# Linear attention with a gated feed-forward on one core: the sums of phi(k) apart from v, w1 and w2 loaded by columns, another order of steps

## The chip, the cores and the metric

The kernel runs on one core of a Trainium2 chip. The metric is the device time of one execution in microseconds (us). Differences of about 2% are what a measurement of this kernel tells from none. Five engines work side by side, each through its own queue of instructions in order: TensorE (PE) multiplies matrices and writes PSUM; VectorE (DVE) and ScalarE (ACT) compute elementwise; GpSimd (POOL) and SyncE (SP) are used here mainly to issue transfers.

## The reference

```
phi(x) = (x if x > 0 else exp(x) - 1) + 1
q_p, k_p = phi(q), phi(k)                     # (8, 8, 576, 64) each
kv  = einsum('bhsd,bhse->bhde', k_p, v)
z   = sum(k_p, axis=2)
att = einsum('bhsd,bhde->bhse', q_p, kv) / (einsum('bhsd,bhd->bhs', q_p, z) + 1e-06)
x   = att with heads joined                   # (4608, 512)
out = ((x @ w1) * (x @ w2) @ w3) @ w_out      # w1, w2: 512x1024, w3: 1024x1024, w_out: 1024x512
```

Inputs and output are float32; the kernel multiplies in bfloat16.

## The kernel before

**Work.** First w3 and w_out are multiplied into one matrix, w_f: for each of eight 128-row pieces of w3, eight transposes on PE (`wt`, L193), a copy out of PSUM (`wc`, L197), eight matmuls with w_out (`wm`, L203) and a copy to bf16 (`wd`, L207). For each batch, q, k and v are loaded in f32 into tiles `raw` of one pool with five buffers, which w3 shares. phi is an exp on ScalarE (`x`, L217), a max and add (`y`, L221) and a min (`z`, L228) on VectorE. v is cast to bf16 next to a column of ones (`vc`, L234), so that one K step (`kv_mm`, L247) gives kv and z together.

**Two ways through attention.** Batches 0 and 1 transpose q on PE (`qa`, `qb`), spread kv and z over 64 columns (`kvz_copy`, L328), multiply both with q (`e`, L339), take the reciprocal as exp(-ln) on ScalarE (`er`, L347 and L348) and multiply (`em`, L352), which leaves x transposed in `xt`. Their last 64 rows go by `rm` and `rd`. Batches 2 to 7 transpose q by DMA (`T`, L260), multiply (`A`, L272: nd), divide (`G`, L290 to L294) and transpose the result into `xt` by DMA (`D`, L306).

**Feed-forward.** The 4608 rows make nine chunks of 512. For each chunk c and each of eight feature blocks f, `g` multiplies x with w1 (a) and w2 (b), four 128-row pieces of the contraction each (L388); ScalarE copies a out of PSUM (`fc`, L399), VectorE multiplies it with b (`fm`, L406 or L408). `O` multiplies with w_f (L416), `oc` copies (L420), `S` stores (L427). The last output piece (`Q`) goes in two parts (L438, L439).

**Order.** A string of steps is written out by hand or by a planner; each step is issued as it stands, and each engine keeps that order. `g0.3.1.0` is chunk 0, block 3, w2, first half of the contraction. A plus sign takes VectorE instead of ScalarE for a copy, and POOL's queue instead of SP's for a load.

**Transfers.** POOL issues the loads that change the type, and in the first stage all of them; eight of its transfers may be in flight, the ninth waits for the first. SP issues later loads, DMA transposes and stores, also eight in flight. A load also waits until its buffer is given back.

**PSUM.** Four buffers of one bank (`mm_ps`) serve w_f, a, b and O; two of two banks (`at_ps`) serve the transposes and attention.

Of the kernel before, what the change touches and what calls it, by code (L numbers as in the profile page):

```python
# [9 lines left out]
F32 = mybir.dt.float32  # L10
# [57 lines left out]
"""


@with_exitstack
def kernel(
# [45 lines left out]
    zero = consts.tile([P, NCH], BF16)  # L118

# [10 lines left out]
    def constants(part):  # L130
        if part == 0:
            make_identity(nc, ident)
        elif part == 1:
            for t in vts:
                nc.vector.memset(t[:, :, :, :, D:D + 1], 1.0)
            nc.vector.memset(eps, 1e-6)
        elif part == 2:
# [14 lines left out]
    def load_qkv(name, src, b, part, pool):  # L152
        if (name, b) not in raw:
            raw[name, b] = ld.tile([P, 4, HW], F32, tag="ld", name=f"{name}32")
        hs = slice(2 * part, 2 * part + 2) if part < 2 else slice(0, 4)
        (nc.gpsimd if pool else nc.sync).dma_start(
            out=raw[name, b][:, hs, :],
            in_=src[b].rearrange("(hp u) (p j) d -> (u p) hp (j d)", u=2, j=NJ)[:, hs, :])
# [79 lines left out]
    def kv_mm(b, cs):  # L238
        if 0 in cs:
            kvps[b] = at_ps.tile([P, 2, NCH], F32, tag="at", name="kvp")  # L240
        kk, vt = ph["k", b], vts[b % 2]
        for c in cs:
            for j in range(NJ):
                for u in range(2):
                    rows = slice(u * R, (u + 1) * R)
                    for a in range(2):
                        nc.tensor.matmul(  # L247
                            kvps[b][a * D:(a + 1) * D, u, c * (D + 1):(c + 1) * (D + 1)],
                            kk[rows, c, j, a, :], vt[rows, c, j, a, :],
                            start=(j == 0), stop=(j == NJ - 1))  # L250
# [73 lines left out]
    def kvz_copy(b, z, alt):  # L324
        t = kvz[b, z] = att.tile([P, 2, 2, D], BF16, tag="kvz", name="kvz", bufs=2)
        src = kvps[b][:, :, 0:2 * (D + 1)].rearrange("p u (c e) -> p u c e", e=D + 1)
        src = src[:, :, :, D:D + 1].to_broadcast([P, 2, 2, D]) if z else src[:, :, :, 0:D]
        copy_of(alt)(out=t, in_=src)  # L328
# [16 lines left out]
    def first_recip(b, c, a):  # L345
        r = rcs[b, c, a] = sm.tile([P, NCH], F32, tag="a_sb", name="rc")
# [98 lines left out]
    def step(s):  # L445
# [32 lines left out]
        elif op == "K":  # L478
            kv_mm(x, (0, 1) if y == 2 else (y,))
        elif op == "kc":  # L480
# [13 lines left out]
        elif op == "kz":  # L494
            kvz_copy(x, y, alt)
# [60 lines left out]
```

## Time and profile before

| what | value |
|---|---|
| median of 3 runs | 252.36 us (252.0 to 255.04) |
| the profiled execution's own time | 252.82 us |
| its span | 251.0 us |
| PE busy | 234.2 us, 93% |
| DVE busy | 152.0 us, 61% |
| ACT busy | 119.7 us, 48% |
| POOL busy | 22.0 us, 9% |
| read from HBM, written | 38.80 MB, 9.44 MB |
| granted PE clock, mean | 0.984 |

The span runs from the first to the last recorded instruction; the time is somewhat longer than the span, since it holds what lies around it. A busy PE isn't PE at its peak, since its matmuls overlap.

### The profile page before, as it was taken

What the parts mean: (1) busy time and instruction counts of PE and PEld (TensorE: products, weight loads), DVE (VectorE), ACT (ScalarE), POOL (GpSimd) and SP (SyncE); (2) the same over time, 40 slices, a digit from 0 to 9 for tenths busy, and PEclk for the clock granted to TensorE, in tenths of its full rate; (3) what the DMA queues carried; (4) which work ended last, traced back from release to release, by engine and by line L of the source; (5) the groups of instructions that cost most, each with busy time, mean ns of one, the idle gap of its engine ahead of it and who ended that gap; (6) DMA issues with size and microseconds to landing.
All of it is one profiled execution on the core that took longest, in us unless ns stands there. A gap on an engine that the chain in (4) does not pass through costs nothing.

```text
span 251.0 us, 4536 instructions
## 1 busy us (share of the span) xinstructions
PE 234.2 (93%) x1799; PEld 112.6 (45%) x1816; DVE 152.0 (61%) x285; ACT 119.7 (48%) x171; POOL 22.0 (9%) x39
## 2 busy tenths in 40 slices
PE   6599888999888999979999999999999999999993
PEld 2255434453443445434444544454444444444442
DVE  0239676987677888686688893576136435633411
ACT  2008898689667773363568773311131233013320
POOL 8651641100000000000000000000000000000000
PEclk9589999999999999999999999999999999999999
DMA  5999999998999997996999942589601201161025
GB/s 101 195 304 386 227 329 336 369 305 160 360 396 188 365 305 154 316 220 147 375 308 343 376 108 73 62 152 138 209 24 33 93 0 55 61 201 42 3 78 131
DMA packets 47796, 50.36 MB, mean 201 GB/s; under 512 B 30496, under 2 KB 30752, under 8 KB 47776
## 3 DMA queue, kind: packets, MB, share of 16 engines
q1 hardware_dynamic: 42272, 34.12, 51.1%
q0 software_dynamic: 5360, 15.86, 22.1%
q8 instruction: 14, 0.23, 0.4%
q10 hardware_dynamic: 144, 0.10, 0.1%
q14 instruction: 6, 0.05, 0.1%
HBM read 38.80 MB, written 9.44 MB: 192 GB/s over the span
## 4 chain that ended last, share of the span: by engine, by line
PE 74%; DMA 17%; issue 2%; ACT 2%; POOL 2%; DVE 1%; SPq 0%; DVEq 0%; ACTq 0%; POOLq 0%
PE b_ps L388 22%; PE a_ps L388 21%; PE o_ps L416 21%; DMA w_sb<-in_moe_w_dram 6%; PE wf_ps L203 5%; DMA q<-in_q_dram 5%; DMA xt<-xn 3%; DMA wo<-in_moe_w_out_dram 3%; PE nd L272 3%; PE kvp L247 2%; ACT e L217 1%; DMA out_dram<-o_sb 1%; PE w3p L193 1%; DVE xt L352 1%; POOL w3b L182 0%
## 5 line engine op out<-in xcount | busy, mean ns | idle before, releaser
L388 PEld LDWEIGHTS <-w_sb 128*128 128x128 bf16 x576 | 54.4, 98 | 67.3 <-issue 4.5
L388 PE MATMUL a_ps<-xt,w_sb 128*128 128x512 bf16 x288 | 70.9, 379 | 2.7 <-DMA xt<-xn 1.4
L388 PE MATMUL b_ps<-xt,w_sb 128*128 128x512 bf16 x288 | 70.2, 379 | 1.2 <-DMA w_sb<-in_moe_w_dram 0.8
L399 ACT COPY a_sb<-a_ps 128x512 f32<-128x512 f32 x72 | 41.7, 584 | 60.1 <-PE a_ps L388 44.1
L408 DVE TENSOR_TENSOR ab<-a_sb,b_ps 128x512 bf16<-128x512 f32 x64 | 45.5, 729 | 32.0 <-ACT a_sb L399 16.9
L416 PE MATMUL o_ps<-wf_sb,ab 128*128 128x512 bf16 x267 | 63.1, 379 | 0.7
L416 PEld LDWEIGHTS <-ab 128*128 128x128 bf16 x280 | 26.8, 98 | 31.8 <-issue 0.6
L217 ACT ACTIVATE e<-k 128x1152 bf16<-128x1152 f32 x16 | 18.1, 1160 | 20.2 <-PE wf_ps L203 16.8
L420 ACT COPY o_sb<-o_ps 128x512 f32<-128x512 f32 x20 | 11.7, 584 | 32.8 <-PE o_ps L416 26.6
L420 DVE COPY o_sb<-o_ps 128x512 f32<-128x512 f32 x15 | 10.3, 690 | 16.6 <-PE o_ps L416 10.2
L217 ACT ACTIVATE e<-q 128x1152 bf16<-128x1152 f32 x16 | 18.1, 1160 | 4.8 <-DMA q<-in_q_dram 3.3
L203 PE MATMUL wf_ps<-wo,w3t 128*128 128x512 bf16 x61 | 16.0, 411 | 1.0 <-DVE w3t L197 0.5
L294 DVE TENSOR_TENSOR xn<-nd,r 128x512 bf16<-128x512 f32 x24 | 15.4, 685 | 0.0
L221 DVE TENSOR_SCALAR r<-k 128x1152 bf16<-128x1152 f32 x16 | 11.9, 751 | 4.2 <-DMA k<-in_k_dram 4.2
L234 ACT CAST vt<-v 128x1152 bf16<-128x1152 f32 x10 | 11.6, 1172 | 2.8 <-PE kvp L247 1.6
L221 DVE TENSOR_SCALAR r<-q 128x1152 bf16<-128x1152 f32 x16 | 11.9, 751 | 0.2
L228 DVE TENSOR_TENSOR k<-e,r 128x1152 bf16<-128x1152 bf16 x16 | 11.8, 748 | 0.0
L228 DVE TENSOR_TENSOR q<-e,r 128x1152 bf16<-128x1152 bf16 x16 | 11.8, 751 | 0.0
L272 PE MATMUL nd<-kvb,qt 128*128 128x130 bf16 (+1 forms) x120 | 10.6, 222 | 1.0 <-DVE xnr L294 1.0
L272 PEld LDWEIGHTS <-qt 128*128 128x128 bf16 (+1 forms) x120 | 8.3, 100 | 7.1 <-issue 2.1
L197 DVE COPY w3t<-w3p 128x1024 bf16<-128x1024 bf16 x6 | 4.0, 688 | 11.8 <-PE w3p L193 11.8
L406 DVE TENSOR_TENSOR ab<-a_sb,b_ps 128x512 bf16<-128x512 f32 x8 | 5.5, 687 | 8.3 <-PE b_ps L388 7.5
(53 smaller groups left out, 128.8 us busy)
## 6 DMA issues: line engine op xcount, KB each, us to landing
out_dram<-o_sb SPq DMA_DIRECT2D x70, 128.0 KB, 2.1
k<-in_k_dram SPq DMA_DIRECT2D x5, 1152.0 KB, 6.4
v<-in_v_dram SPq DMA_DIRECT2D x5, 1152.0 KB, 9.6
q<-in_q_dram SPq DMA_DIRECT2D x5, 1152.0 KB, 10.3
k<-in_k_dram POOLq DMA_DIRECT2D x4, 576.0 KB, 10.6
q<-in_q_dram POOLq DMA_DIRECT2D x4, 576.0 KB, 10.4
v<-in_v_dram POOLq DMA_DIRECT2D x4, 576.0 KB, 13.5
w3b<-in_moe_w_dram POOLq DMA_DIRECT2D x8, 256.0 KB, 9.0
```

The costliest lines, as they stand in the source:

```text
L203: nc.tensor.matmul(wfs[i], w3ts[i][:, kc, :], wos[0][:, kc, :], start=(kc == 0), stop=(kc == FC - 1))
L217: nc.scalar.activation(out=es[name, b, c], in_=raw[name, b][:, 2 * c:2 * c + 2, :], func=AF.Exp)
L221: nc.vector.tensor_scalar(out=rs[name, b, c], in0=raw[name, b][:, 2 * c:2 * c + 2, :], scalar1=0.0, scalar2=1.0, op0=ALU.max, op1=ALU.add)
L228: nc.vector.tensor_tensor(out=ph[name, b][:, c].rearrange("p j a d -> p a j d"), in0=es[name, b, c].rearrange("p a (j d) -> p a j d", j=NJ ...
L234: copy_of(alt)(out=vts[b % 2][:, c, :, :, 0:D].rearrange("p j a d -> p a j d"), in_=raw["v", b][:, 2 * c:2 * c + 2, :].rearrange("p a (j d ...
L272: nc.tensor.matmul(nd[0:n, u, 2 * c * (D + 1):2 * (c + 1) * (D + 1)], w, kvb[b % 2][:, u, c].rearrange("p a e -> p (a e)"), start=True, st ...
L294: nc.vector.tensor_tensor(out=dst.rearrange("p (i u) e -> p u i e", u=2), in0=v4[:, :, :, 0:D], in1=r[0:n].unsqueeze(3).to_broadcast([n, 2 ...
L388: nc.tensor.matmul(fps[c, f, w], (w1_sb, w2_sb)[w][:, kc, f * P:(f + 1) * P], xt[:, 4 * c:4 * c + 4, kc, :], start=(first and n == 0), sto ...
L399: nc.scalar.copy(out=fsb[c, f], in_=fps[c, f, 0])
L408: nc.vector.tensor_tensor(out=abs_[c][:, f].rearrange("p (m t g) -> p m g t", g=2, t=R), in0=fsb[c, f].rearrange("p (m g t) -> p m g t", g ...
L416: nc.tensor.matmul(o_pss[c, m], abs_[c][:, f, m * P:(m + 1) * P], wf_sb[:, f, :], start=(f == 0), stop=(f == FC - 1))
L420: copy_of(alt)(out=o_sbs[c, m], in_=o_pss[c, m])
```

## The change

1. For batches 0 and 1 (`SUMS_FIRST`) v is loaded as bf16 by the transfer itself, and its cast (`vc`) is gone. K uses it as it lies in the raw tile, with 64 columns instead of 65.
2. The sums z are computed by a step of their own, `Z` (36 matmuls for each half batch against a tile of ones), which needs k only. `kvz_copy` is split into halves (`kz b.z.c`), z from the new sums' PSUM tile, kv from K's.
3. The reciprocals of batches 0 and 1 lie in the tiles of `xn` instead of the small pool `a_sb`.
4. w1 and w2 are loaded in halves of columns (features 0 to 511, then 512 to 1023) instead of halves of rows.
5. The order is a new one from end to end. At its head q of batch 0 comes first, its first half on SP's queue, with 9, 11 and 1 warm-up matmuls instead of 10, 4 and 6; chunk 0 works blocks 0 to 3, then 4 to 7. Later K, A, G and D of batches 2 to 7 stand at other places, and k and v of batch 4 are loaded ahead of batch 3.

```diff
+    ones = consts.tile([P, D], BF16)
...
+            if name == "v" and b in SUMS_FIRST:
+                raw[name, b] = raw[name, b].bitcast(BF16).rearrange("p h x -> p (h x)")[:, 0:4 * HW].rearrange(
+                    "p (h x) -> p h x", h=4)
...
     def load_w12(x, y):
-        kcs = slice(2 * y, 2 * y + 2)
+        fs = slice(y * NCH, (y + 1) * NCH)
         nc.gpsimd.dma_start(
-            out=(w1_sb, w2_sb)[x][:, kcs, :],
-            in_=(moe_w1, moe_w2)[x].rearrange("(c p) n -> p c n", p=P)[:, kcs, :])
+            out=(w1_sb, w2_sb)[x][:, :, fs],
+            in_=(moe_w1, moe_w2)[x].rearrange("(c p) n -> p c n", p=P)[:, :, fs])
...
-        kk, vt = ph["k", b], vts[b % 2]
+        kk = ph["k", b]
+        if b in SUMS_FIRST:
+
+            n, vt = D, raw["v", b].rearrange("p (c a) (j d) -> p c j a d", a=2, j=NJ)
+        else:
+            n, vt = D + 1, vts[b % 2]
...
+    def z_mm(b, c):
+
+        if b not in zps:
+            zps[b] = at_ps.tile([P, 2, NCH], F32, tag="at", name="zp")
+        kk = ph["k", b]
+        for j in range(NJ):
+            for u in range(2):
+                rows = slice(u * R, (u + 1) * R)
+                for a in range(2):
+                    nc.tensor.matmul(zps[b][a * D:(a + 1) * D, u, c * D:(c + 1) * D],
+                                     kk[rows, c, j, a, :], ones[rows], start=(j == 0), stop=(j == NJ - 1))
+
+    def kvz_copy(b, z, c, alt):
+        if (b, z) not in kvz:
+            kvz[b, z] = att.tile([P, 2, 2, D], BF16, tag="kvz", name="kvz", bufs=2)
+        cs = slice(c, c + 1) if c < 2 else slice(0, 2)
+        if z and b in zps:
+            src = zps[b][:, :, 0:2 * D].rearrange("p u (c e) -> p u c e", e=D)[:, :, cs]
...
+        copy_of(alt)(out=kvz[b, z][:, :, cs], in_=src)
```

The head of the two orders (loads `l`, with `w` for w1 and w2, `e` for w3, `o` for w_out):

```
before  i2 i1 le6 lo1 H10 le0 lo0 le7 le3 lo3 i0 lo2 wt6 le5 wt0 wc6+ lk0.1+ wc0+ lq0.0+ wm6.0.4 i3 wm0.0.4 le1 ...
        ... lw0.1 ... lw0.0 ... lk1.0+ ... lq1.0+ ... lw1.0 ... lk1.1+ ... lw1.1 ...
after   i2 lq0.0 le2 i1 lo0 H9 i0 i3 lo1 le3 le6 le0 wt2 H11 lo2 wc2+ xq0.0 lo3 yq0.0 le1 zq0.0 lk0.0+ qa0.0 le5 ...
        ... lw0.0 ... lk1.1+ ... lk1.0+ ... lw1.0 ... lq1.0+ ... lw0.1 ... lq1.1+ ... lw1.1 ...
```

Places in the new order that the prediction speaks of:

```
... e1.0.0 er1.1.1 em1.1.0 O0.3 em1.0.1 xq2.1 em1.0.0 O0.0 ... zq2.0 xk2.1 S0.0 g1.1.0.1 ... fc1.1 ...
... A3.2 fm2.0 A3.3 xq4.1 O1.3 G3.1 xq4.0 O2.2 oc1.3 D2.2 yq4.0 D3.1 ... O2.3 ... g3.7.0.2 ...
... S1.2 kc4.1+ fc3.3 zq5.0 A4.1 A4.0 g3.2.1.2 G4.0 T5.0 ... D4.0 ... g4.2.0.2 ...
```

More of the change, by code (lines that the diff above doesn't have):

```diff
@@ new lines @@
+wm6.4.8 lv0.1+ wd2+ wt1 wd6+ wm0.4.8 lw0.0 wc1 yk0.0 wm3.4.8 xk0.0 wd0+ lk1.1+ wt5 wd3+ wm1.0.4 wc5 zk0.0
+lk1.0+ wm1.4.8 xk0.1 yk0.1 wm5.0.4 wd1+ wm5.4.8 zk0.1 lw1.0 xq0.1 Z0.0 wd5+ Z0.1 lq1.0+ yq0.1 kz0.1.0 wt4
+kz0.1.1 wc4+ e0.0.1 lw0.1 er0.0.1 zq0.1 wt7 wm4.0.4 wc7+ lq1.1+ er0.0.0 wm4.4.8 qa0.1 lw1.1 wd4 K0.0 qb0.1+
+wm7.0.4 kz0.0.0+ e0.1.1 e0.0.0 er0.1.0 K0.1 em0.0.0 wm7.4.8 em0.0.1 lv1.1+ kz0.0.1 er0.1.1 e0.1.0 wd7+
+g0.2.0.0 em0.1.0 g0.1.0.0 lv1.0+ g0.0.0.0 xk1.1 em0.1.1 rm0 g0.3.0.0 yk1.1 rd0 lq2.2+ g0.2.0.1 yk1.0
@@ new lines @@
+er1.1.1 em1.1.0 O0.3 em1.0.1 xq2.1 em1.0.0 O0.0 yq2.0 oc0.3 xq2.0 S0.3 yq2.1 g1.1.1.0 em1.1.1 g1.1.0.0 oc0.0
+g1.0.1.0 zq2.0 xk2.1 S0.0 g1.1.0.1 g1.7.0.0 zq2.1 g1.7.0.1 fc1.1 g1.1.1.1 yk2.1 T2.0 rm1 fc1.7 fm1.1
+g1.4.0.0 xk2.0 g1.6.1.0 zk2.1 g1.7.1.0 rd1 g1.4.0.1 T2.1 vc2.1+ g1.6.1.1 g1.0.1.1 fc1.4 yk2.0 g1.7.1.1 vc2.0
+g1.6.0.0 zk2.0 g1.6.0.1 lk4.2 fm1.7 K2.0 fc1.6 lv4.2 K2.1 fm1.6 g1.2.0.0 lk3.2 kc2.0 g1.3.0.0 kc2.1+
+g1.4.1.0 A2.0 A2.1 g1.2.0.1 G2.0 g1.4.1.1 fc1.2 g1.3.0.1 g1.2.1.0 fc1.3 g1.2.1.1 g1.3.1.0 fm1.4 A2.2 A2.3
@@ new lines @@
+zq5.0 A4.1 A4.0 g3.2.1.2 G4.0 T5.0 g3.0.0.2 g3.3.1.2 fm3.2 D4.0 K5.0 K5.1 fm3.3 fc3.0 g3.6.1.2 S1.3 kc5.0
+fm3.0 A4.2 g3.7.1.2 kc5.1+ S2.1 A4.3 fm3.7 g3.6.0.2 T5.1 G4.1 g4.2.0.2 fc3.6 g4.2.1.2 fc4.2 g4.5.0.2 lv6.2
+fm4.2 g4.3.0.2 lq6.2 fc4.5 fm3.6 g4.0.0.2 lk6.2 fc4.3 O3.1 fc4.0 A5.0 oc3.1+ O3.0 A5.1 oc3.0 g4.1.0.2 G5.0
+S3.1 g4.5.1.2 vc6.0 g4.0.1.2 D4.1 fm4.5 g4.3.1.2 fm4.0 fc4.1 g4.6.0.2 D5.0 fm4.3 xq6.1 A4.4 g4.6.1.2 G4.2
+g4.7.1.2 fc4.6 yq6.0 xq6.0 O3.3 yq6.1 lq7.2 xk6.0 fm4.6 g4.1.1.2 oc3.3+ lk7.2 xk6.1 A5.4 O3.2 fm4.1 S3.3
@@ new lines @@
+G5.2 g4.7.0.2 D4.2 oc3.2 zq6.0 g5.7.0.2 vc6.1+ fc4.7 g5.4.0.2 yk6.1 fc5.7 A5.2 fm4.7 fc5.4 g4.4.0.2 D5.2
+zq6.1 g4.4.1.2 fc4.4 zk6.1 T6.1 xq7.0 g5.3.0.2 fm4.4 g5.3.1.2 xq7.1 yq7.0 O4.2 yq7.1 T6.0 fc5.3 zq7.0 xk7.1
+O4.3 fm5.3 oc4.2 S3.2 yk7.1 xk7.0 zq7.1 g5.7.1.2 S4.2 zk7.1 oc4.3 g5.2.0.2 fm5.7 g5.2.1.2 S4.3 fc5.2 yk7.0
+g5.6.0.2 fm5.2 S3.0 g5.5.1.2 fc5.6 zk7.0 g5.4.1.2 lv7.2 yk6.0 A5.3 g5.0.0.2 fm5.4 T7.1 zk6.0 O4.1 fc5.0 G5.1
+T7.0 g5.0.1.2 g5.5.0.2 fm5.0 K6.0 fc5.5 D5.1 oc4.1+ K6.1 g5.6.1.2 fm5.5 kc6.1 S4.1 kc6.0 g5.1.1.2 vc7.0
@@ new lines @@
+fm5.6 A6.2 A6.3 vc7.1 g5.1.0.2 G6.1 O4.0 fc5.1 fm5.1 D6.1 A6.0 K7.0 oc4.0+ K7.1 O5.1 kc7.0 S4.0 kc7.1 A6.1
+oc5.1 O5.3 G6.0 S5.1 O5.0 oc5.3+ D6.0 A7.4 oc5.0+ A7.1 S5.3 O5.2 G7.2 S5.0 A7.0 oc5.2 g6.4.0.2 G7.0 D7.2
+g6.3.1.2 fc6.4 S5.2 g6.0.0.2 g6.1.0.2 fc6.0 D7.0 g6.0.1.2 fc6.1 g6.4.1.2 fm6.0 g6.2.0.2 fm6.4 g6.1.1.2 fc6.2
+g6.6.1.2 fm6.1 g6.3.0.2 g6.7.0.2 fc6.3 fm6.3 g6.2.1.2 fc6.7 g7.2.0.2 fm6.2 g6.6.0.2 fc7.2 g7.7.0.2 fc6.6
+fm6.6 g7.3.0.2 fc7.7 g7.2.1.2 g6.7.1.2 fm7.2 g7.6.1.2 fc7.3 fm6.7 g6.5.1.2 g7.6.0.2 g7.4.0.2 fc7.6 fm7.6
@@ L68 @@
+fm8.1 O7.3 fc8.0 fm8.0 O8.0 oc7.3 S7.3 O8.1 oc8.0 S8.0 O8.2 oc8.1 S8.1 oc8.2 S8.2 Q8.3
 """
+SUMS_FIRST = (0, 1)
 @with_exitstack
@@ L136, in constants @@
             nc.vector.memset(eps, 1e-6)
+            nc.vector.memset(ones, 1.0)
         elif part == 2:
@@ L322, in q_copy @@
         copy_of(alt)(out=qts[b][:, :, c], in_=tqs[b, c].rearrange("p (j u t) -> p u j t", u=2, t=R))
[L324 to L328, printed above, removed]
+    zps = {}
+    def z_mm(b, c):
[14 more added lines that the diff above has]
+            src = zps[b][:, :, 0:2 * D].rearrange("p u (c e) -> p u c e", e=D)[:, :, cs]
+        else:
+            src = kvps[b][:, :, 0:2 * (D + 1)].rearrange("p u (c e) -> p u c e", e=D + 1)[:, :, cs]
+            src = src[:, :, :, D:D + 1].to_broadcast([P, 2, cs.stop - cs.start, D]) if z else src[:, :, :, 0:D]
+        copy_of(alt)(out=kvz[b, z][:, :, cs], in_=src)
     def first_mm(b, c, z):
@@ L345, in first_recip @@
     def first_recip(b, c, a):
-        r = rcs[b, c, a] = sm.tile([P, NCH], F32, tag="a_sb", name="rc")
+        if b in zps:
+            if (b, c) not in rcs:
+                rcs[b, c] = att.tile([P, NG, H, D], BF16, tag="xn", name="rc").bitcast(F32).rearrange(
+                    "p j h d -> p (j h d)")
+            r = rcs[b, c][:, a * NCH:(a + 1) * NCH]
+        else:
+            r = sm.tile([P, NCH], F32, tag="a_sb", name="rc")
+        rcs[b, c, a] = r
         nc.scalar.activation(out=r, in_=nd1[b, c, 1][a], func=AF.Ln, bias=eps[:, 0:1])
@@ L479, in step @@
             kv_mm(x, (0, 1) if y == 2 else (y,))
+        elif op == "Z":
+            z_mm(x, y)
         elif op == "kc":
```

74 lines of the change are left out of this document (24 added, 50 removed).

## The prediction

> **What bounds the kernel now.** I read the page first, then the busy time by stage, then the chain of waits in order of time, and the transfers last.
>
> ```profile
> span 251.0 us, 4536 instructions
> ...
> PE 234.2 (93%) x1799; PEld 112.6 (45%) x1816; DVE 152.0 (61%) x285; ACT 119.7 (48%) x171; POOL 22.0 (9%) x39
> ```
>
> TensorE (PE) is busy 93% of the span, so only the rest, slow matmuls and added matmuls can move the time. Where the rest lies is read from the stages (columns: PE, PEld, DVE, ACT, POOL busy, PE clock, DMA share, GB/s) and from the chain.
>
> ```profile
> 0.00:5.00 5.00, 3.72 (x10) 1.33 (x11) 0.45 (x4) 1.28 (x1) 3.96 (x11) 1.00 0.51 83
> 5.00:10.00 5.00, 1.71 (x17) 1.37 (x17) 0.98 (x2) 0.00 (x0) 3.51 (x8) 0.75 1.06 182
> 10.00:15.00 5.00, 4.83 (x24) 2.43 (x23) 1.00 (x2) 0.00 (x0) 3.24 (x6) 0.57 1.12 218
> ...
> 53.40:62.40 9.00, 8.89 (x57) 3.78 (x59) 7.20 (x11) 8.32 (x13) 0.00 (x0) 1.00 0.97 177
> ```
>
> ```profile
> 9.94 3.57 PE wf_ps L203 x8
> ...
> 18.77 0.45 PE w3p L193 x8
> ...
> 28.78 14.17 DMA w_sb<-in_moe_w_dram
> 43.00 3.20 PE b_ps L388 x14
> ...
> 52.69 0.71 PE kvp L247 x70
> 53.40 0.32 PE o_ps L416
> ...
> 55.23 0.50 PE tq L316 x9
> ...
> 59.63 0.37 PE nd L339 x4
> ...
> 82.12 2.59 PE a_ps L388 x12
> ...
> 104.84 7.06 DMA xt<-xn
> ...
> 112.04 1.02 PE a_ps L388 x4
> 113.06 0.86 PE b_ps L388 x4
> ```
>
> To compare two orders I use a **debt**: the time at which PE reaches a step, less the matmul work queued ahead of it at full clock. Prices are 0.86/4 = 0.216 us for a 512-column matmul, 0.45 for eight transposes of w3, 0.50 for nine of q, 0.36 for half of a K step (0.71/2), 0.37 for an e step. Ahead of the first output product (53.40) the order has 20 warm-ups, 64 w_f and 64 FFN matmuls (148 x 0.216 = 32.0), 8 w3 steps (3.6), 3 q steps (1.5), 4 K halves (1.4), 4 e steps (1.5) and the rest of batch 0 (0.2): 40.1 us. The debt is 13.3. At the first FFN matmul of chunk 2 (82.12) the same count gives 65.3, debt 16.8; at chunk 3 (112.04) 93.4, debt 18.6. The last matmul is this:
>
> ```profile
> 245.13 1.91 PE L438 MATMUL o_ps<-wf_sb,ab 128*128 128x320 bf16 x16
> ```
>
> PE ends at 247.0 after 226.4 of work, debt 20.6. Two thirds of all debt is there by 53 us, and the chain says why: all of w2's second matmuls wait until 43.00 for the last half of w2. After 112 it grows by only 2.0.
>
> The head is paced by transfers. POOL issues them; the landing follows by adding the latency of each:
>
> ```profile
> 1.24 0.68 POOL L182 DMA_DIRECT2D w3b<-in_moe_w_dram  x1 [0.80 <-POOLq L540]
> ...
> 48.44 0.75 POOL L156 DMA_DIRECT2D v<-in_v_dram  x1 [5.71 <-ACT e L217]
> ```
>
> ```profile
> w3b<-in_moe_w_dram POOLq DMA_DIRECT2D x1, 256.0 KB, 3.6
> ...
> v<-in_v_dram POOLq DMA_DIRECT2D x1, 1152.0 KB, 9.0
> ```
>
> The first POOL transfer lands at 4.84, the 31st at 57.4. Between them 20.6 MB are read (f32 in memory: 0.52 for a w3 or w_out piece, 0.59 for half a batch, 1.05 for half of w1 or w2): 0.392 MB/us, with DMA at 1.0 in the stages above.
>
> **The change part by part.**
>
> *Fewer bytes ahead of the first useful pairs.* Before, an a product needs both row halves of w1 and a b product both of w2. With column halves, features 0 to 3 need one half of each. In the new POOL order 13.1 MB land up to w2's first half, 16.4 up to its second, 17.6 up to v of batch 1. At the rate above: 4.84 + 12.6/0.392 = 36.9, 45.3 and 48.3 us. The new PE order has 29.5 us of work ahead of the step that needs the first of them (101 matmuls of 0.216, eight w3, two q, two Z, two K and four e steps, the rest of batch 0), and counted alike 38.5 and 41.1 ahead of the others: debts of 7.4, 6.8, 7.2. q's first half now goes by SP's queue, whose first work before was this:
>
> ```profile
> 53.33 1.37 SPq L260 DMA_TRANSPOSE qt<-q  x1
> ```
>
> So it may start before POOL's; the stream is earlier by 0 to 1.5 us (all its bytes). Against that stands what the engines need between landings, walked on the earlier stream. w_out's last piece lands at 14.2 (4.3 MB after the first), with 10.3 of work ahead: debt 3.9. From there to the first FFN matmul PE has 15.5 of work and waits only for hand-offs (PSUM buffers, kvz): 1.0 more. Then four a products fill all four PSUM buffers until ScalarE copies them out, behind four logarithm pairs and two exps of k:
>
> ```profile
> 30.57 0.69 ACT L347 ACTIVATE rc<-nd,eps 128x512 f32<-128x512 f32 x1 [0.51 <-PE nd L339]
> 31.29 0.63 ACT L348 ACTIVATE rc<-rc 128x512 f32<-128x512 f32 x1
> ```
>
> The first copy ends about 1.0 after the fourth product: 6.0 at the first output product, if the stream is early, 7.4 if it isn't. I take **7.0**.
>
> *POOL's waits.* The two halves of k of batch 1 wait for PE (the w3 buffer), later q and k of batch 2 too; what stands behind them are the halves of w1 and w2. PE gives the first buffer back after 12.5 us of work, near 17, when the ring of eight transfers in flight lets that issue go only at 19.9. Covered by 3 us; without that, each us is one of debt.
>
> *The cold clock.* The stages from 5 to 15 us show clocks of 0.75 and 0.57, and eight w_f matmuls took 3.57 (0.45 each). The new order puts 11 warm-ups between the first w3 step and q's transposes, so that these can run at 0.216. That is 1.8 us inside the walk above; if the clock falls again, w_out's last piece (15.7 us by the stream) hides most of it. If it shows (a rival below), it is those 1.8.
>
> *Added PE work.* Z steps: 2 x 72 matmuls of the K shape, 2 x 0.71 = 1.4; one more warm-up, 0.2. The total is 228.1.
>
> *Casts of v.* Four are gone (two per engine):
>
> ```profile
> 26.73 1.17 ACT L234 CAST vt<-v 128x1152 bf16<-128x1152 f32 x1
> ...
> 27.72 0.92 DVE L234 CAST vt<-v 128x1152 bf16<-128x1152 f32 x1 [0.43 <-DMA v<-in_v_dram]
> ```
>
> About 2.3 of ScalarE and 1.7 of VectorE; four more narrow kvz copies give back about 1. Off the path except where an engine is full (below). The loads themselves read the same 0.59 MB and write half. Bounds: 0.75 us each if the written bytes set it, 1.5 if the read ones. The casting loads of w3 keep the read rate, so I take 1.5: no gain.
>
> *Pieces of w1 and w2.* Rows of 4 KB become 2 KB, 512 pieces instead of 256 for each half.
>
> ```profile
> q1 hardware_dynamic: 42272, 34.12, 51.1%
> q0 software_dynamic: 5360, 15.86, 22.1%
> ```
>
> Share x span x 16 / packets: 48.5 ns for 0.81 KB, 166 ns for 2.96 KB, so 54 ns per KB and 4.6 ns per packet. 256 more packets over 16 engines are 0.07 us for each half. Bounds 0 and 2.7 (time per piece unchanged); I take 0.1. The Trainium skill (DMA: Bandwidth & Descriptors, Why small descriptors are slow) has about three fixed cycles for each packet; as an estimate, 35 beats against half of 67 is 4.5%, 0.5 us on four halves; the sum would be 0.1 to 0.2 higher.
>
> *Chunk 1.* From the first output product to the second division of batch 2 (G2.1) the order holds 18.7 us of PE work and, by the rows below, on VectorE 12 steps of 0.75 or less (8.4), 6 products of 0.73 (4.4), 3 of 0.69 (2.1) and two G steps, each two of 0.69 with small ones to 1.85 (3.7): 18.6.
>
> ```profile
> L408 DVE TENSOR_TENSOR ab<-a_sb,b_ps 128x512 bf16<-128x512 f32 x64 | 45.5, 729 | 32.0 <-ACT a_sb L399 16.9
> ...
> L294 DVE TENSOR_TENSOR xn<-nd,r 128x512 bf16<-128x512 f32 x24 | 15.4, 685 | 0.0
> ...
> L221 DVE TENSOR_SCALAR r<-k 128x1152 bf16<-128x1152 f32 x16 | 11.9, 751 | 4.2 <-DMA k<-in_k_dram 4.2
> ```
>
> Before, VectorE was 80% busy there (7.20 of 9.00). Two engines full at once wait for each other; I take 2.5 (0.5 to 4): **9.5** at chunk 2. Also, exp of k of batch 2 stands on ScalarE ahead of chunk 1's copies, which free PSUM; k lands at 54.3, its turn comes near 55.4. This is what is late next: beyond 1 us of delay PE pays.
>
> *Chunks 3 and 4.* Before, from the last nd ahead of it (A3.0, 100.84) to the landing (111.9) took 11.1 us, with 9.6 of PE work as cover. Now A3.3 to chunk 3 has 8.9: a wait of 2.2, **11.9** with switches. For chunk 4 the cover is 6.4; the chain is G4.0 (1.85 and 0.5 of queue), T5.0 ahead of it on SP (1.4) and the transpose:
>
> ```profile
> xt<-xn SPq DMA_TRANSPOSE x12, 5.1
> ...
> xt<-xn SPq DMA_TRANSPOSE x1, 8.6
> ```
>
> With 5.1 it is 8.9, a wait of 2.5; with few loads in flight less. I take 1.2: **13.1**. Then the growth of before, a little less: 1.8, **14.9**. Other reorderings move matmuls with the same prices and stand in that growth.
>
> *Sum.* 228.1 + 14.9 + (252.82 - 247.0, what lies behind the last matmul and around the span, unchanged) = 248.8. The profiled execution is 0.46 above the median of the runs shown: **248.3**.
>
> **The rivals.**
> *All kept (244.4).* The debt grows after the first output product by 4 only: the casts freed VectorE, and the clean stretch of before grew 2.0 in 135 us. Against: the DVE count above. 228.1 + 11.0 + 5.8 - 0.5.
> *Given back at chunk 4 (253.0), slower than before.* One transpose, D4.0, stands behind T5.0 and S1.2 on SP. If it lands as chunk 3's did while loads streamed (8.6 from issue, above), the chain is 12.3 against 6.4: 5.9 instead of 1.2. Decisive from a landing of about 8 us on. For: chunk 3's wait of 7.06. Against: few loads are queued there.
> *The clock falls again (250.1).* If q's first half lands after the 11 warm-ups are done (near 8 us), PE idles as it did from 5 to 10 us: 1.71 busy, then a clock of 0.57. The price is the 1.8 above. Against: q is the first transfer on its queue. The Trainium skill (TensorE: Matmul & The Clock Gate, Part 1) states that about 3.4 us of idling halve the clock; the two stage rows agree.
> *Pieces cost as before (258).* Each half of w1 and w2 takes 2.7 more; 10.7 by the last. 248.3 less a us of cover plus 10.7. Against: the packet prices.
> *It does not shorten the head (254).* ScalarE's chain of logarithms, not w1 and w2, sets the first FFN matmul; then only the 1.6 of added PE work is left. Against: the 14.17 of the chain.
>
> **How the numbers follow.** Forecast 0.52 (own range 246 to 251; a third of it below 247.3), all kept 0.23, given back 0.13, the clock 0.05, pieces 0.04, no shorter head 0.03. A measurement of this kernel can tell about 2% from no change: 247.3 and 257.4. Faster: 0.17 + 0.23 = 0.40; slower, the pieces: 0.04; within: 0.56. The range, 244 to 253.5, takes in the bounds of chunk 1, the given-back case and most of all kept.
>
> **What would show it.** First output product near 50.6 us (right between 49 and 52), clock 1.0 from about 4 us on, w2's second half landing near 45; chunk 2 near 81, chunk 3 near 108, with xt's transposes ahead of chunks 3 and 4 in the chain. Wrong if the chain shows k or v of batch 2, if w1's halves land over 3 us apart without anything between, or if the first output product comes after 53.

## The result, and the profile after

| kernel | median | runs |
|---|---|---|
| before | 252.18 us | 4 runs, 251.95 to 255.04 |
| changed | 248.12 us | 4 runs, 247.56 to 250.99 |

The ratio is 0.9857 (95% interval 0.9809 to 0.9905): 1.4% faster, which is less than the 2% that a measurement of this kernel tells from none by itself. Two repeats below have 0.9878 and 0.9859. The forecast was 248.3. Its time was right and two of its terms were not, by about 4 us each, with opposite signs. The profiled execution of the changed kernel is the slowest of its four (250.99), so a second profile of the same kernel (the first experiment, median 248.19, span 246.2) stands beside it wherever the two differ.

The page of the changed kernel, rows as shown of before:

```profile
span 248.8 us, 4827 instructions
...
PE 237.5 (95%) x1961; PEld 113.9 (46%) x1961; DVE 149.0 (60%) x280; ACT 120.2 (48%) x177; POOL 22.2 (9%) x38
...
q0 software_dynamic: 6752, 14.09, 22.7%
```

PE idles for 11.3 us of the span instead of 16.8, but it is busy for 3.3 more: 1.6 is added work, and its 11 warm-ups alone took 2.3 more than at full clock. POOL's queue (the last row) has 1392 packets more than before: 1024 more from the halves of columns (5728 packets in the run with halves of rows), 512 more from the loads of v in bf16 (6240 in the run with v in f32), and 144 less because q's first half left this queue. Its share of time went from 22.1% to 22.7%; what the halves of columns cost is read below, where only they differ.

The busy time by stage (PE, PEld, DVE, ACT, POOL busy, PE clock, DMA share, GB/s):

```profile
5.00:10.00 5.00, 2.28 (x12) 1.29 (x12) 1.00 (x2) 0.53 (x1) 3.28 (x7) 1.00 0.95 160
10.00:15.00 5.00, 5.00 (x23) 2.29 (x22) 1.80 (x3) 0.00 (x0) 3.05 (x5) 1.00 1.12 210
...
56.00:85.10 29.10, 28.57 (x229) 13.56 (x229) 24.84 (x49) 22.98 (x30) 0.00 (x0) 1.00 0.80 234
85.10:111.50 26.40, 25.17 (x197) 11.64 (x195) 20.33 (x40) 13.38 (x19) 0.00 (x0) 1.00 1.05 258
111.50:140.00 28.50, 28.35 (x285) 14.02 (x286) 18.51 (x39) 12.15 (x19) 0.00 (x0) 1.00 0.91 242
```

PE idles for 1.2 us at the start, 2.7 between 5 and 10 us, 1.9 from 15 to 56, 0.5 up to chunk 2 and 1.2 before chunk 3, and hardly after until its last matmul ends at 245.2. From 10 to 15 us it is full with only 23 matmuls. The clock column says 1.00 there, and it is wrong: the durations below say half. This execution's first clock record is at 13.8 us, and nothing ahead of it was known.

The chain of waits, in order of time:

```profile
1.25 6.64 DMA w3b<-in_moe_w_dram
...
7.93 1.03 PE w3p L202 x8
8.96 4.69 PE warm L152 x11
13.66 0.62 PE tq L330 x9
...
54.39 1.02 PE b_ps L428 x4
55.42 0.56 PE nd L372 x8
55.97 1.19 PE o_ps L456 x5
...
85.14 3.45 PE a_ps L428 x16
...
89.47 0.46 SPq L274
...
89.98 3.92 SPq L274
...
93.96 0.58 SPq L165
...
94.58 10.03 DMA v<-in_v_dram
...
105.63 5.75 DMA xt<-xn
...
111.51 1.89 PE a_ps L428 x8
```

The 14.17 of w1 and w2 that stood in the chain of before is gone. What the kernel now waits for in the head is the first w3 piece: 6.64 us instead of 3.6. Behind it stand 11 warm-ups at 0.43 each, on the path. The first output product comes at 55.97, later than before (53.40), with 3.5 us more work ahead of it. Ahead of chunk 3 the chain runs over v of batch 5, whose load stands on SP behind two transposes of q: VectorE comes to the cast of that v (`vc5.0+`), waits for it until 104.64, and the last transfer into xt is issued only at 105.63.

The landings of w1 and w2, by issue and latency (first, w2's first half, w1's second, w2's second):

```profile
w_sb<-in_moe_w_dram POOLq DMA_DIRECT2D x1, 512.0 KB, 11.6
w_sb<-in_moe_w_dram POOLq DMA_DIRECT2D x1, 512.0 KB, 12.7
w_sb<-in_moe_w_dram POOLq DMA_DIRECT2D x1, 512.0 KB, 13.1
w_sb<-in_moe_w_dram POOLq DMA_DIRECT2D x1, 512.0 KB, 15.3
```

They were issued at 19.7, 24.0, 27.5 and 29.3, so they land at 31.3, 36.7, 40.6 and 44.6. The forecast had 36.9 and 45.3 for w2's halves.

### The profile page after: what moved, and what is told of

Its sections match the earlier page's. It is cut to its first block, busy times and chain, and to the rows that moved or that the text cites. A ratio compares the mean times of both kernels' runs of the same rounds, so it can differ in the third digit from the quotient of the medians.

```text
span 248.8 us, 4827 instructions
## 1 busy us (share of the span) xinstructions
PE 237.5 (95%) x1961; PEld 113.9 (46%) x1961; DVE 149.0 (60%) x280; ACT 120.2 (48%) x177; POOL 22.2 (9%) x38
## 3 DMA queue, kind: packets, MB, share of 16 engines
q0 software_dynamic: 6752, 14.09, 22.7%
## 4 chain that ended last, share of the span: by engine, by line
PE 80%; DMA 10%; DVE 3%; ACT 2%; SPq 2%; issue 2%; DVEq 0%; POOLq 0%
PE a_ps L428 23%; PE b_ps L428 21%; PE o_ps L456 20%; PE wf_ps L212 5%; DMA v<-in_v_dram 4%; PE nd L286 3%; DMA w3b<-in_moe_w_dram 3%; DMA xt<-xn 2%; PE warm L152 2%; SPq L274 2%; PE kvp L261 2%; PE w3p L202 1%; DMA out_dram<-o_sb 1%; PE tq L330 1%; PE nd L372 1%
## 5 line engine op out<-in xcount | busy, mean ns | idle before, releaser
L428 PE MATMUL a_ps<-xt,w_sb 128*128 128x512 bf16 x288 | 69.7, 379 | 1.2 <-DMA xt<-xn 1.2
L448 DVE TENSOR_TENSOR ab<-a_sb,b_ps 128x512 bf16<-128x512 f32 x64 | 45.8, 729 | 33.2 <-PE b_ps L428 19.7
L456 PE MATMUL o_ps<-wf_sb,ab 128*128 128x512 bf16 x280 | 64.1, 379 | 0.0
L460 ACT COPY o_sb<-o_ps 128x512 f32<-128x512 f32 x24 | 14.0, 585 | 32.9 <-PE o_ps L456 31.4
L212 PE MATMUL wf_ps<-wo,w3t 128*128 128x512 bf16 x64 | 15.3, 380 | 0.4 <-ACT w3t L206 0.2
L308 DVE TENSOR_TENSOR xn<-nd,r 128x512 bf16<-128x512 f32 x24 | 15.4, 683 | 0.0
L460 DVE COPY o_sb<-o_ps 128x512 f32<-128x512 f32 x11 | 7.6, 687 | 7.4 <-PE o_ps L456 7.2
L286 PE MATMUL nd<-kvb,qt 128*128 128x130 bf16 (+1 forms) x120 | 11.1, 222 | 0.2
L206 ACT COPY w3t<-w3p 128x1024 bf16<-128x1024 bf16 x4 | 4.0, 1012 | 14.8 <-PE w3p L202 14.8
L152 PE MATMUL warm<-zero 128*128 128x512 bf16 x21 | 9.3, 621 | 1.2 <-DVE zero L144 1.2
## 6 DMA issues: line engine op xcount, KB each, us to landing
w_sb<-in_moe_w_dram POOLq DMA_DIRECT2D x4, 512.0 KB, 12.9
```

The lines of the kernel that those rows point to most:

```text
L152: nc.tensor.matmul(ps, zero[:, 0:P], zero, start=True, stop=True)
L212: nc.tensor.matmul(wfs[i], w3ts[i][:, kc, :], wos[0][:, kc, :], start=(kc == 0), stop=(kc == FC - 1))
L286: nc.tensor.matmul(nd[0:n, u, 2 * c * (D + 1):2 * (c + 1) * (D + 1)], w, kvb[b % 2][:, u, c].rearrange("p a e -> p (a e)"), start=True, st ...
L308: nc.vector.tensor_tensor(out=dst.rearrange("p (i u) e -> p u i e", u=2), in0=v4[:, :, :, 0:D], in1=r[0:n].unsqueeze(3).to_broadcast([n, 2 ...
L428: nc.tensor.matmul(fps[c, f, w], (w1_sb, w2_sb)[w][:, kc, f * P:(f + 1) * P], xt[:, 4 * c:4 * c + 4, kc, :], start=(first and n == 0), sto ...
L448: nc.vector.tensor_tensor(out=abs_[c][:, f].rearrange("p (m t g) -> p m g t", g=2, t=R), in0=fsb[c, f].rearrange("p (m g t) -> p m g t", g ...
```

## The experiments

All ratios are to the kernel before on the same chip in the same sitting, whose median was 251.51 for the first four runs, 251.75 for the next four and 252.23 for the last four.

**The changed kernel again.** No edit.

> The changed kernel once more, for a second profile. The first one was its slowest execution (250.99; the other three 247.56 to 248.18): the first piece of w3 landed at 7.9 us, the 20 warm-ups of its start took 427 ns each, and the first output product came at 55.9 (work ahead 43.6, debt 12.3, not 7.0). Theory A (a cold start was this execution's own): a profile near 248 shows a clock at full before 13 us and a first output product near 53, with the same later stages. Theory B (the head is always like that and the runs differ later): first output product at 55.5 to 56 again, and the 3 us elsewhere.

Measured: 248.19, ratio 0.9878 (0.9849 to 0.9907), span 246.2. PE's work in order of time:

```profile
1.19 3.73 PE L152 MATMUL warm<-zero 128*128 128x512 bf16 x9 [1.19 <-DVE zero L144]
7.81 0.97 PE L202 MATMUL w3p<-ident,w3b 128*128 128x128 bf16 x8 [2.88 <-DMA w3b<-in_moe_w_dram]
8.57 3.90 PE L152 MATMUL warm<-zero 128*128 128x512 bf16 x11
12.31 0.67 PE L330 MATMUL tq<-ident,q 128*128 128x128 bf16 x9
...
17.66 2.76 PE L212 MATMUL wf_ps<-wo,w3t 128*128 128x512 bf16 x12 [0.24 <-ACT w3t L206]
...
240.69 1.91 PE L478 MATMUL o_ps<-wf_sb,ab 128*128 128x320 bf16 x16
```

The first output product stands at 54.70, between the marks of the two theories. The late first piece of w3 is not that execution's own; the cold clock is so in part: the 11 warm-ups took 0.35 each here. Of the 2.6 us between the two spans, 1.3 are there at 17.66 (18.96 in the other), and 1.2 are the wait ahead of chunk 3, which this execution does not have.

**A bridge of warm-ups over the wait.**

```diff
-i2 lq0.0 le2 i1 lo0 H9 i0 i3 ...
+i2 lq0.0 le2 i1 lo0 H25 i0 i3 ...
```

> 25 warm-ups instead of 9 before the first w3 step, so that PE stays busy until 8 us. Theory A: the clock rises by 4 to 7.5 us and stays; the 11 warm-ups behind take 2.4 us instead of 4.7, the head is 2 to 3 us earlier than in the cold profile, time 246.5 to 248.0 and no slow executions. Theory B (transfers pace the head whatever the clock is, w_out's last piece at 16.7): within 0.5 us of the changed kernel's 248.1.

Measured: 247.48, ratio 0.9847 (0.9818 to 0.9876), span 244.8.

```profile
1.19 7.14 PE L152 MATMUL warm<-zero 128*128 128x512 bf16 x25 [1.19 <-DVE zero L144]
...
8.61 2.54 PE L152 MATMUL warm<-zero 128*128 128x512 bf16 x11
11.10 0.68 PE L330 MATMUL tq<-ident,q 128*128 128x128 bf16 x9
...
16.46 2.76 PE L212 MATMUL wf_ps<-wo,w3t 128*128 128x512 bf16 x12 [0.24 <-ACT w3t L206]
```

The clock is full from its first record at 4.4 us until PE's work is done, the 11 warm-ups take 0.23 each, and what stands behind them is 1.2 us earlier than in the repeat, and so to the end of the kernel. That is Theory A by the trace; the medians, 0.7 us apart, would not decide alone. Against 2.54, the 11 warm-ups' 3.90 in the repeat and 4.90 in the profile after put the price of the cold clock at 1.4 and 2.4 us.

**The changed head with the old order behind it, and the other way round.** In the first, the order is the new one up to `g1.1.1.0`, then the old one without what is done. In the second it is the old one up to `g1.7.0.0`, with v in f32, no Z and halves of rows, then the new one.

> The changed kernel's steps up to the first FFN product of chunk 1, then the order of before. If the head brought the gain, as predicted (6 us of debt less 1.6 of added work): 247 to 249.5. If the order behind it did (debt grew by 4.6 instead of 7.3 in the profiled executions): 250.5 to 252.5.

> The steps of before up to the first FFN product of chunk 1, with w1 and w2 in halves of rows, v loaded in f32 and no sums apart, then the changed kernel's order. If the head brought the gain: 251 to 253.5. If the order behind it did: 248.5 to 250.

Measured: 260.22 (ratio 1.0347, 1.0301 to 1.0393) and 249.46 (0.992, 0.9894 to 0.9945). The first missed every expectation. Its SP, VectorE and PE, in order of time:

```profile
63.30 2.06 SPq L467 DMA_DIRECT2D out_dram<-o_sb  x2
65.53 0.46 SPq L165 DMA_DIRECT2D k<-in_k_dram  x1
```

```profile
71.21 0.76 DVE L230 TENSOR_SCALAR r<-k 128x1152 bf16<-128x1152 f32 x1 [5.63 <-DMA k<-in_k_dram]
```

```profile
73.04 0.62 PE L286 MATMUL nd<-kvb,qt 128*128 128x130 bf16 x4 [5.01 <-DVE xnr L308]
```

The old order has k of batch 3 on SP behind two transposes of q and stores of chunk 0, which the new head reaches later (that k is issued at 65.53, before at 59.97); VectorE stands behind that k, and PE behind VectorE for 5.0 us, after which the granted clock is 0.72 from 70 to 82 us. A second load of k costs 7.8 us in the chain at 124. The old order can't stand behind the new head as it is: its order of loads on SP is fitted to the head in front of it. So this run doesn't tell what the new head is worth alone. The second came out where the gain lies behind the head (248.5 to 250): the new order there is worth 0.8% alone, by the ratios more than half of the whole gain, with its wait for xt ahead of chunk 3 (6.78 in its chain).

**Fewer warm-ups behind the first w3 step.**

```diff
-i2 lq0.0 le2 i1 lo0 H9 i0 i3 lo1 le3 le6 le0 wt2 H11 lo2 wc2+ xq0.0 ...
+i2 lq0.0 le2 i1 lo0 H25 i0 i3 lo1 le3 le6 le0 wt2 H3 lo2 wc2+ xq0.0 ...
```

> The changed order with 25 warm-ups ahead of the first w3 step instead of 9, and 3 behind it instead of 11 (the run with 25 and 11 gave 247.48, its q transposes at 11.10 us). Theory A (from the landing of the first w3 piece on, near 7.8 us, the head is one chain of work on PE, and the warm-ups behind it stand in it): eight matmuls of 0.216 less, 1.7 us; q transposes near 9.4, span near 243, time 245.8 (245.3 to 246.8). Theory B (landings pace the head from there on: w3, w_out, q): the next w3 or w_out piece takes the place of the warm-ups, 247.0 to 247.8.

Measured: 248.13, ratio 0.9879 (0.9827 to 0.9931). Nothing is gained, and neither theory has the reason:

```profile
8.72 0.81 PE L152 MATMUL warm<-zero 128*128 128x512 bf16 x3
11.38 0.68 PE L330 MATMUL tq<-ident,q 128*128 128x128 bf16 x9 [1.84 <-DVE q L237]
```

```profile
8.93 0.69 DVE L206 COPY w3t<-w3p 128x1024 bf16<-128x1024 bf16 x1 [7.41 <-PE w3p L202]
9.53 0.92 DVE L230 TENSOR_SCALAR r<-q 128x1152 bf16<-128x1152 f32 x1
10.57 0.76 DVE L237 TENSOR_TENSOR q<-e,r 128x1152 bf16<-128x1152 bf16 x1
```

In VectorE's queue the copy of the first w3 step (`wc2+`) stands ahead of phi of q (`yq0.0`, `zq0.0`). q landed at 4.3 and its exp was done at 5.5, but VectorE waits 7.41 us for the w3 piece first. So q's transposes come 3.1 us after the first w3 step (8.28 to 11.38), and 2.9 us in the run with 11 warm-ups at full clock in between (8.17 to 11.10).

**q's first half on POOL's queue.**

```diff
-i2 lq0.0 le2 i1 lo0 H9 ...
+i2 le2 i1 lo0 lq0.0+ H9 ...
```

> The changed kernel with the first half of q of batch 0 on POOL's queue behind w_out's first piece, instead of on SP's queue ahead of all (changed kernel again: 248.19). Theory A (q's half, 0.59 MB from 0.74 us on, is what makes the first w3 piece land at 7.8 instead of 4.84): first w3 step near 5 us, q transposes still behind q's phi near 10.5, so 1 to 2 us off: 246.7 (246 to 247.5). Theory B (the first w3 piece lands late for a reason of its own, such as the transfers issued right behind it): first w3 step still near 7.8, everything behind q's half on POOL 0.5 to 1.3 later: 248.5 to 249.7.

Measured: 247.5, ratio 0.9847 (0.9802 to 0.9892).

```profile
5.00 1.06 PE L202 MATMUL w3p<-ident,w3b 128*128 128x128 bf16 x8
5.86 2.81 PE L152 MATMUL warm<-zero 128*128 128x512 bf16 x11
10.87 0.68 PE L330 MATMUL tq<-ident,q 128*128 128x128 bf16 x9 [2.21 <-DVE q L237]
```

Theory A: without q beside it the first w3 piece is there at 5.0 instead of 7.8, so q's transfer is what delayed it. The Trainium skill (DMA: Bandwidth & Descriptors, Queues, rings and completion order) has each engine take turns between the queues that have work for it; this pair of runs agrees. The gain is small because q now lands at 8.8 and q's transposes wait for its phi: the twelve w_f matmuls of 17.66 in the repeat stand at 16.23.

**Halves of rows in the new order.**

```diff
-        fs = slice(y * NCH, (y + 1) * NCH)
+        kcs = slice(2 * y, 2 * y + 2)
...
-            out=(w1_sb, w2_sb)[x][:, :, fs],
+            out=(w1_sb, w2_sb)[x][:, kcs, :],
```

> The changed kernel with w1 and w2 in halves of rows as before, order unchanged. Theory A (the prediction: 2 KB rows cost no more by themselves, and with row halves every a product needs w1's second piece): that piece lands near 40.6, while PE has done the first halves of four a products at 36.8 (changed kernel again): a wait of 3.8, part of it given back later: 251.0 to 252.2, and landings of the four pieces within 1 us of the changed kernel's. Theory B (2 KB rows cost 1 us or more for each piece): landings of the four pieces 1 to 10 us earlier, and 247.5 to 250.

Measured: 254.38, ratio 1.0116 (1.0074 to 1.0159).

```profile
36.62 0.61 PE L428 MATMUL a_ps<-xt,w_sb 128*128 128x512 bf16 x2
41.55 3.50 PE L428 MATMUL a_ps<-xt,w_sb 128*128 128x512 bf16 x8 [4.33 <-DMA w_sb<-in_moe_w_dram]
45.72 2.75 PE L428 MATMUL b_ps<-xt,w_sb 128*128 128x512 bf16 x12 [0.67 <-ACT a_sb L439]
```

The place of Theory A, at a price that it missed. The wait is 4.33, and the eight matmuls behind it take 3.50 instead of 1.73: the granted clock is 0.66 from 41 to 46 us. Together 6.1, which is the whole difference of 6.2 to the repeat; nothing is given back. The Trainium skill (TensorE: Matmul & The Clock Gate, Part 1) puts the idle time that halves the clock at about 3.4 us, and this wait agrees. But 3.4 us in one piece are not needed: before the change the clock is 0.75 from 5 to 10 us, and PE's longest idle stretch there is 2.27 us. The pieces of 4 KB rows land no sooner (w1's second half at 41.5; in the repeat 40.9), so in the landings rows of 2 KB cost nothing that can be seen. POOL's queue is busy for 22.0% of this span of 252.1 us and 23.0% of the repeat's 246.2: 1.2 us more on 16 engines for the 1024 packets, 0.3 for each half.

**v in f32 with casts, Z kept.**

```diff
+... er0.0.0 vc0.0 wm4.4.8 qa0.1 lw1.1 vc0.1+ wd4 K0.0 ...
+... g0.5.1.1 vc1.0+ fc0.6 ... g0.6.1.0 vc1.1 fm0.7 ... K1.0 ...
```

> The changed kernel with v of batches 0 and 1 loaded in f32 and cast by four instructions as before (two on ScalarE, two on VectorE); the sums ahead of v and the order are kept. Theory A (the prediction: casts stand beside other work and the load of bf16 lands no sooner): 248.2, within 0.6 of the changed kernel. Theory B (the casts stand in the head's chain, or the bf16 load is sooner by up to 0.75 each): 249.5 to 252.

Measured: 249.47, ratio 0.9882 (0.9827 to 0.9937). Not decided: by the ratios 0.1 to 0.6 us more than the repeats of the changed kernel (0.9878 and, below, 0.9859), with intervals of 1.4 us to each side. The one cost that PE shows in the head, in the profile of an execution of 253.31 us, is

```profile
32.97 0.48 PE L258 MATMUL kvp<-vt,k 64*64 64x64 bf16 x36 [0.52 <-ACT vt L240]
```

**phi of q first.** What the runs with few warm-ups and with q on POOL point to:

```diff
-... H9 i0 i3 lo1 le3 le6 le0 wt2 H11 lo2 wc2+ xq0.0 lo3 yq0.0 le1 zq0.0 lk0.0+ qa0.0 le5 wm2.0.4 qb0.0+ ...
+... H20 i0 i3 lo1 le3 le6 le0 xq0.0 yq0.0 zq0.0 qa0.0 qb0.0+ wt2 H4 lo2 wc2+ lo3 le1 lk0.0+ le5 wm2.0.4 ...
```

> The changed order with phi of q of batch 0, its transposes and their copy ahead of the first w3 step's copy on VectorE, and with 20 and 4 warm-ups instead of 9 and 11. Theory A (in the head the chain is: first w3 step near 8 us, its copy, then phi of q on VectorE, then q's transposes, then w_f; the run with 3 warm-ups behind showed q's transposes waiting for phi): q's transposes near 7, first w_f matmuls near 9.7 instead of 11.6 (long warm-up) or 12.8 (changed kernel again). The second w3 piece then comes next, near 11.4: so 0.9 to 1.1 less than with the long warm-up, 246.4 (245.8 to 247.2). Theory B (landings of w3 and w_out pace the head from 12 us on anyway): 247.2 to 248.2.

Measured: 246.13 (245.74 to 246.61), ratio 0.9759 (0.9722 to 0.9796), the fastest of all.

```profile
7.27 0.67 PE L330 MATMUL tq<-ident,q 128*128 128x128 bf16 x9
...
9.39 1.04 PE L212 MATMUL wf_ps<-wo,w3t 128*128 128x512 bf16 x4
10.67 0.62 PE L202 MATMUL w3p<-ident,w3b 128*128 128x128 bf16 x8 [0.24 <-DMA w3b<-in_moe_w_dram]
11.92 0.62 PE L202 MATMUL w3p<-ident,w3b 128*128 128x128 bf16 x8 [0.63 <-DMA w3b<-in_moe_w_dram]
```

As Theory A had it, down to the next wait: now w3's second and third pieces come last. It is 2.5 us below the changed kernel beside it (the last run).

**Z twice.** Each Z step is written twice in a row.

> The changed kernel with each of the four steps that sum phi(k) run twice in a row: 144 more matmuls of the K shape. Theory A (from 16 us on the head is PE's own work with short waits, so added work shows in full): four times 0.355 to 0.41, 1.4 to 1.6 more than the changed kernel of the same job. Theory B (the steps stand where PE waits for w1, w2 or hand-offs): 0 to 0.7 more.

Measured: 248.93, ratio 0.9893 (0.984 to 0.9945), 0.3 more than the changed kernel beside it by the medians and 0.9 by the ratios, with intervals of 1.1 and 1.3 us to each side: the times don't decide. In the traces each batch's added steps cost 0.6. PE is 0.9 us ahead of the other profile at the twelve w_f matmuls (15.71 against 16.61, since its warm-ups ran at full clock), 0.3 ahead behind batch 0's steps (33.74 against 34.05) and 0.3 late behind batch 1's (43.46 against 43.17). Then PE stops at 45.58 for 1.34 us, for which the profile names no cause, and the first output product comes at 55.62 instead of 53.80. But chunk 3 starts at 109.72 instead of 109.88, since the wait of 1.7 for xt that the other profile has there is gone. So the added work costs nearly its price where it stands, and a wait behind it can take it back.

**Column halves alone, in the old order.**

```diff
-            out=(w1_sb, w2_sb)[x][:, kcs, :],
+            out=(w1_sb, w2_sb)[x][:, :, fs],
...
-... lw0.1 ... lw0.0 ... g0.0.0.0 em0.1.1 g0.6.0.0 lv1.1+ g0.5.0.0 ... g0.3.0.0 ...
+... lw0.0 ... lw0.1 ... g0.0.0.0 em0.1.1 g0.1.0.0 lv1.1+ g0.2.0.0 ... g0.3.0.0 ...
```

> The kernel before with w1 and w2 in halves of columns, w1's first half first, and chunk 0's blocks renamed so that the four that the order takes first are features 0 to 511; nothing else is changed. Theory A (the halves are worth what the old order waits for them): the wait of 0.84 at 43.00 goes, and no other comes: 0 to 1 less than before, ratio 0.996 to 1.0. Theory B (the halves are the gain of the whole change, whatever the order): ratio 0.98 to 0.988. If 2 KB rows cost, the ratio is over 1.002.

Measured: 252.18, ratio 1.0009 (0.997 to 1.0048). Neither gain nor cost: Theory A with no gain, and not Theory B. The profiled execution took 852.3 us, so no trace shows whether the wait of 0.84 went.

**The changed kernel once more.**

> The changed kernel once more, beside the others of this job, as the base of their differences: 248.2 (247.5 to 249), ratio 0.984 to 0.988. Both theories say the same here; the repeat shows whether its first stage again has the first w3 step near 7.8 us and warm-ups that run at half clock for a part.

Measured: 248.63, ratio 0.9859 (0.9817 to 0.9901), span 247.2. Its chain:

```profile
92.22 10.33 DMA v<-in_v_dram
...
103.53 6.22 DMA xt<-xn
...
109.88 1.89 PE a_ps L428 x8
```

The first w3 step is at 7.09, the 11 warm-ups take 0.32 each, the first output product stands at 53.80, 0.9 earlier than in the first repeat, and chunk 3 at 109.88, 0.9 later. One kernel, three profiles: a wait ahead of chunk 3 of 1.2, none and 1.7. In all three the last transfer into xt ahead of chunk 3 is issued about 1.0 us after v of batch 5 has landed (landing at 104.6, 101.6 and 102.6, issue at 105.63, 102.67 and 103.53).

## Why the prediction was right, and where it was not

Time at which PE reaches each mark; the debt (time less work ahead, as defined there) in brackets:

| mark | work ahead | forecast | profile after | again | once more |
|---|---|---|---|---|---|
| first output product | 43.6 | 50.6 (7.0) | 55.97 (12.4) | 54.70 (11.1) | 53.80 (10.2) |
| chunk 2 | 71.7 | 81.2 (9.5) | 85.14 (13.4) | 83.87 (12.2) | 82.81 (11.1) |
| chunk 3 | 96.1 | 108.0 (11.9) | 111.51 (15.4) | 109.03 (12.9) | 109.88 (13.8) |
| end of the last matmul | 228.1 | 243.0 (14.9) | 245.22 (17.1) | 242.60 (14.5) | 243.59 (15.5) |

Before, these debts were 13.3, 16.8, 18.6 and 20.6. So the change took 0.9 to 3.1 us off in the head, and 2.0 to 3.9 behind it, where the debt grew by 3.4 to 5.3 instead of 7.3; 1.6 is paid for the added work.

*The head: wrong, 7.0 against 10.2 to 12.4.* The failing step is "debt 3.9" at w_out's last piece. At the twelve w_f matmuls in a row (17.66 in the repeat, 9.4 of work ahead) it is 8.2: 5.9 from the first w3 piece (7.81, with 1.9 of work ahead), 1.4 from cold warm-ups, 0.9 from hand-offs. w_out's last piece, for which that step let PE wait, landed at 16.6 in the repeat instead of 14.2, and even then PE was not there. The prediction took the landing of 4.84 from before as the start of the stream and let q's half start "0 to 1.5" us sooner beside it, as a gain; it is what made that piece late, as q on POOL's queue showed. That is not all of it: with the piece at 5.0 the twelve matmuls still stood at 16.23, and with phi of q moved ahead on VectorE at 14.96, though 0.9 more of warm-ups lay in front (the first w3 piece landed at 6.6 there). The walk had no term for VectorE's queue, in which phi of q stood behind the copy of the first w3 step. From 17.66 to the first output product the debt grew by 2.9, as forecast (3.1). By the prediction's own mark, "if the first output product comes after 53", the step is wrong.

*The cold clock: a rival that came true from another cause.* It was given 0.05, if q's half landed late. q was there at 4.3; the w3 piece was late, and PE idled from 5 to 8 us. The price of 1.8 lies between the two that the bridge gives, 1.4 and 2.4.

*Fewer bytes ahead of the first useful pairs: right in its landings, wrong in what it is worth.* The landings of w2's halves were within 0.7 us of the forecast. But the reading that the last half of w2 explains the head's debt was wrong. This is what PE waited for it before:

```profile
43.00 3.20 PE L388 MATMUL b_ps<-xt,w_sb 128*128 128x512 bf16 x14 [0.84 <-DMA w_sb<-in_moe_w_dram]
```

The 14.17 in the chain is the transfer from its issue to its landing, and PE had other work for nearly all of it. Of the debt of 13.3, 8.1 was PE's idle time, 0.84 of that this wait, and 5.2 was busy time above the price of its matmuls. That fits what the halves of columns bring in the old order, nothing (ratio 1.0009). In the new order they are worth 6.2 us, and without them it is slower than the kernel before. They allow the order, whose first four products need only w1's first half; they are no gain by themselves, and no term of a sum.

*Pieces, casts:* by the queue's share each half of w1 and w2 cost 0.3 instead of 0.1, and by the landings nothing; the rival of 2.7 is out. The casts' nothing isn't told from the 0.5 that one of them cost PE.

*Z:* 0.7 for each batch was nearly right where it stands (0.6 when run twice); a wait behind it may take it back.

*Chunk 1: over-sized.* VectorE and ScalarE stood busy, 24.84 and 22.98 of 29.10, and PE lost 0.9 to 1.1 instead of 2.5. *Chunk 3:* forecast 2.4 more, measured 0.8 to 2.7 by execution, at the right place, but over v of batch 5 on SP and not over the chain of A3.3 alone. *Chunk 4 and the rest:* 1.6 to 1.7 together instead of 3.0; PE is busy for 28.35 of the 28.5 us behind chunk 3's start.

So the growth behind the first output product was 3.4 to 5.3 instead of 7.9. That is the 4 of the rival "all kept"; but with the head 3 to 5 us later, its 244.4 was not reached. Two errors of about 4 cancelled. What the forecast got right from its profile were the landings and the place of the wait ahead of chunk 3; the sizes came from bounds whose worst ends it had added up in the middle and left out at the start.

## What to carry to other kernels

Look first at what the first transfer competes with: a second queue's load that starts beside it delays it, even if that load is needed early. (Farther on the two orders are level again: w_out's last piece landed at 16.6, and at 16.4 with q on POOL's queue.) Read what a transfer costs from the idle time of the engine that needs it, and not from its length in the chain. In an engine's in-order queue, put the work whose data is there ahead of work that waits for a transfer; here phi of one half of q, moved past one copy, brought 2.5 us together with a bridge of warm-ups (0.7 of it by the bridge alone), where the whole change had brought 3.6. A change of layout and a change of order can be worth nothing and less than nothing apart (here ratios of 1.0009 and 1.0116), so price them together, and expect a wait downstream to take back part of what the head gains.

## What the runs showed of the hardware

- 0.59 MB on SP's queue from 0.74 us on made a 256 KB casting load on POOL's queue land in 5.4 to 6.8 us, by execution, instead of 3.6.
- Nine warm-ups (1.19 to about 5 us) raise the clock for what follows in some executions only: after 1.9 to 3.3 us of idling the next 11 took 0.43, 0.35, 0.32 and, in the run with Z twice, 0.23 each. With 25 in a row they took 0.23. The Trainium skill (TensorE: Matmul & The Clock Gate, Part 1) speaks of a free-running window of time that must be busy, which fits that the same start comes out cold or warm.
- The profile's clock column reads 1.00 ahead of the first clock record (at 13.8 us in the profile after), also where a 512-column matmul takes 0.43 us instead of 0.216. Durations decide.
